# In a seven-product block multiply, the first product is copied by ScalarE into the PSUM bank of another, with two smaller moves around it

## The chip, the cores and the metric

The kernel runs on one NeuronCore of one Trainium2 chip. The metric is device time in microseconds (us) for one execution; lower is better. Three timed runs of the kernel before gave 754.74, 755.83 and 756.22 us; the median, 755.83 us, is what a predicted time is compared with.

## The reference, cut to what matters

The reference is one transformer block: linear attention with a memory, then a gated MLP on its output `h` (2048 rows, 1024 columns). Only the second part matters here:

```
z  = gelu(layernorm(h) @ w_in)            # 2048 x 3584
z1 = z[:, :1792]
z2 = layernorm(z[:, 1792:])               # over the 1792 columns
g  = w_sp @ z2 + b_sp                     # w_sp is 2048 x 2048
out = h + (z1 * g) @ w_out
```

The change lies in the calculation of `z1`, and in the row normalization of `z2` that is done beside it.

## The kernel before, in words

Every instruction is recorded in program order, given to one engine's queue, and supplied with semaphore waits from what it reads and writes (class `_Recorder`, lines 34 to 241; L210, the line all instructions carry in the profile, is the one that emits them). There is no scheduler: each engine runs its instructions strictly in the order in which the code below records them. A whole PSUM bank counts as one cell, so a matmul that adds to a bank waits until every earlier reader of that bank on another engine is done.

**The stage before: z2.** TensorE runs 64 groups of 8 matmuls of 448 columns, ScalarE applies gelu to each (`z2_gelu`, 826), VectorE takes the statistics (`z2_stats`, 830), and GpSimd turns a row's variance into its inverse root with two small instructions (`zrs`, 835 and 836). Side jobs are hung on numbered groups by `at(q, ...)` (994); among them the first weight sums on GpSimd (lines 1016 and 1017).

**The stage of the change: z1, a seven-product block multiply** (`z1_step`, 1199). A 2 x 2 block product is made of seven half-depth products instead of eight. A group `g` (there are 14: 7 column blocks for each of 2 row pairs) has the products 1 to 7; each is four matmuls of 512 columns, with sums of weight blocks as stationary operand (`sz_sum`, 985, GpSimd, tiles `sz`) and differences of activation blocks as moving one (`hn_sum`, 972, VectorE, tiles `ht`). Below, "5 of 9" is product 5 of group 9. A group has three PSUM banks:

- bank 0: product 1, then product 2 added by TensorE; ScalarE applies gelu out of the bank.
- bank 1: product 6, then 7, then 4 added by TensorE.
- bank 2: product 5, then product 3 added.

Product 1 is needed in all four output blocks. The kernel before copies it to SBUF (ScalarE, `s1`, line 1213) and VectorE adds it three times: `u2 = bank 1 + s1` after product 6 (1215); `u3 = bank 1 + s1` and `u3 = bank 2 + u3` after product 7 (1220, 1221); `s1 = bank 1 + s1` after product 4 (1230). A fifth add, `u2 = bank 2 + u2`, comes after product 3 (1233). ScalarE makes each finished block a bf16 block of `z1T` with a gelu (`z1_out`, 1194).

**The order of the products** is written by hand in line 1262:

```
offs = {1: -5, 6: 0, 5: 1, 7: 3, 2: 4, 4: 6, 3: 12}
for x, g, k in sorted((7 * g + offs[k], g, k) for g in range(14) for k in offs):
```

The steady order is 6 of g, 5 of g, 1 of g+1, 7 of g, 2 of g, 3 of g-1, 4 of g, then 6 of g+1. At the opening, where the earlier groups are missing, it is 1, 6, 5 of group 0, 1 of group 1, 7, 2, 4 of group 0, 6 of group 1. Banks are taken in turn from eight (`next_bank`, 421).

The weight sums 1 and 2 of group g+1 are recorded after product 5 of g, sum 3 after product 7, and sum 4 of group g+2 after product 3. The tiles of sums 1 to 3 are single, so sum 1 of a group waits until TensorE has done product 5 of the group before.

**Side jobs of z1** are hung on products by `on(g, k, ...)` (1240). They are: for g of 0 to 7 the normalization of two rows of `z2` (`z2_apply`, 839), one on VectorE after product 6 and one on ScalarE after product 4 (line 1245; the ScalarE form needs a small GpSimd instruction, `znm`, 842, first); in groups 4 to 7 the activation differences of the second row pair; in groups 8, 9 and 11 the scaling of three blocks of `w_sp` on ScalarE, four pieces each, after products 6, 7, 2 and 4 (`sp_part`, 1057, tiles `b11h`, `b12h`, `b22h`); in groups 10 to 13 their differences on VectorE (`sp_sum`, tiles `t1h`, `t2h`, `t3h`). The raw `w_sp` blocks come by transposing DMAs on SP's queue (1250 to 1252).

After z1 comes the gate stage (`gate`, 1087), then the output products.

Of the kernel before, what the change touches and what calls it, by code (L numbers as in the profile page):

```python
# [9 lines left out]
ACTF = mybir.ActivationFunctionType  # L10
ALU = mybir.AluOpType
# [247 lines left out]
def bass_sequential_preLN__memory_aug_infini_attn__mixer_gmlp__prompt_kernel(  # L259
# [17 lines left out]
    pe, act, dve, pool, sp = R.pe, R.act, R.dve, R.pool, R.sp  # L277
# [6 lines left out]
    def tens(name, shape, dt, off):  # L284
        sz = int(np.prod(shape[1:])) * mybir.dt.size(dt)
        assert off % 32 == 0 and off + sz <= ARENA, (name, off, sz)
        t = nc.alloc_sbuf_tensor_at(name, list(shape), dt, offset=abase + off)
        R.space[t[:].tensor.name] = ("sbuf", off)
        return t
# [14 lines left out]
    IDENT = cb("ident", [128, 128], BF16)  # L304
# [73 lines left out]
    ZT = [tens("zt%d" % i, [128, L], F32, o * K) for i, o in enumerate((4, 6, 8, 10, 202, 12))]  # L378
# [30 lines left out]
    PS = nc.alloc_psum_tensor("ps", [128, 8, 512], F32)  # L409
    R.space[PS[:, 0, :].tensor.name] = ("psum", 0)  # L410

    def bank(b):
        return PS[:, b, :]
# [7 lines left out]
    def next_bank():  # L421
        b = rot["banks"][rot["n"] % len(rot["banks"])]
        rot["n"] += 1
        return b
# [367 lines left out]
    for t in range(4):  # L792
        for h in range(2):
            pe.matmul(PS[:, br, t * 128:(t + 1) * 128], RSB[:, h, t:t + 1].to_broadcast([128, 128]), IDENT[:],
                      start=(h == 0), stop=(h == 1))
# [17 lines left out]
    zs, zq, staged = [], [], []  # L813
# [25 lines left out]
    def z2_apply(on_act=False):  # L839
        tc = zq.pop(0)  # L840
        if on_act:
            pool.tensor_scalar(ZNM[:], ZMV[:, tc, 0:1], ZRS[:, 8 * tc:8 * tc + 1], -1.0, ALU.mult, ALU.mult)
            act.activation(Z2H[:, tc, :], Z2[:, tc, :], ACTF.Identity, scale=ZRS[:, 8 * tc:8 * tc + 1], bias=ZNM[:])
            return
        dve.tensor_scalar(Z2H[:, tc, :], Z2[:, tc, :], ZMV[:, tc, 0:1], ZRS[:, 8 * tc:8 * tc + 1], ALU.subtract, ALU.mult)
# [123 lines left out]
    def hb(j, k, p):  # L969
        return HNT[2 * p + k][:, 4 * j:4 * j + 4, :]  # L970
# [7 lines left out]
    def wz_blk(i, j, fc):  # L978
        o = 128 * (fc % 2)
        return WZH[fc // 2][:, 4 * j:4 * j + 4, i, o:o + 128]  # L980

    def sz(g, k):
        return SZ[k - 1 + (k == 4 and g % 2)][:]

    def sz_sum(g, k):
        fc = g % 7
        a, b, op = {1: (wz_blk(1, 0, fc), wz_blk(1, 1, fc), ALU.add), 2: (sz(g, 1), wz_blk(0, 0, fc), ALU.subtract),
                    3: (wz_blk(0, 0, fc), wz_blk(1, 0, fc), ALU.subtract),
                    4: (wz_blk(0, 1, fc), sz(g, 2), ALU.subtract)}[k]
        pool.tensor_tensor(sz(g, k), a, b, op)  # L990
# [3 lines left out]
    def at(q, f, *a):  # L994
        aux.setdefault(q, []).append((f, a))
# [18 lines left out]
    for k in range(4):  # L1014
        at(28 + 2 * k, hn_sum, 1, 1 + k // 2, k % 2)
    for k in (1, 2, 3, 4):
        at(35 + k, sz_sum, 0, k)

    todo = [(0, 2), (0, 3), (0, 8), (0, 9), 0, (0, 10), 1, (0, 11), 2, (1, 0), 3]
    todo += [(1, tc) for tc in range(1, 4)] + [(0, tc) for tc in range(12, NTC)]  # L1020
# [173 lines left out]
    def z1_out(fc, t, src):  # L1194
        act.activation(Z1T[:, fc, t * 512:(t + 1) * 512], src, ACTF.Gelu_apprx_tanh, scale=INV[1][:])

    zb, todo1 = {}, {}

    def z1_step(g, k):
        p, fc = divmod(g, 7)  # L1200
        s1, u2, u3 = ZT[g % 2][:], ZT[2 + g % 3][:], ZT[5][:]
        ka = {1: wz_blk(0, 0, fc), 2: wz_blk(0, 1, fc), 3: sz(g, 4), 4: wz_blk(1, 1, fc), 5: sz(g, 1),
              6: sz(g, 2), 7: sz(g, 3)}[k]
        kb = {1: hb(0, 0, p), 2: hb(1, 0, p), 3: hb(1, 1, p), 4: HT[p][4], 5: HT[p][1], 6: HT[p][2], 7: HT[p][3]}[k]
        first = k in (1, 6, 5)
        r = {1: 0, 2: 0, 6: 1, 7: 1, 4: 1, 5: 2, 3: 2}[k]
        if first:
            zb[g, r] = next_bank()
        b = bank(zb[g, r])
        for i in range(4):  # L1210
            pe.matmul(b, ka[:, i, :], kb[:, i, :], start=(first and i == 0), stop=(i == 3), skip_group_check=True)
        if k == 1:
            act.activation(s1, b, ACTF.Copy)
        if k == 6:
            dve.tensor_tensor(u2, b, s1, ALU.add)
        if k == 5 and g < 13:
            for x in (1, 2):
                sz_sum(g + 1, x)
        if k == 7:
            dve.tensor_tensor(u3, b, s1, ALU.add)  # L1220
            dve.tensor_tensor(u3, bank(zb[g, 2]), u3, ALU.add)
            z1_out(fc + 7, 2 * p + 1, u3)
            if g < 13:
                sz_sum(g + 1, 3)
        if k == 2:
            z1_out(fc, 2 * p, b)
            if g == 0:
                sz_sum(1, 4)
        if k == 4:
            dve.tensor_tensor(s1, b, s1, ALU.add)  # L1230
            z1_out(fc + 7, 2 * p, s1)
        if k == 3:
            dve.tensor_tensor(u2, b, u2, ALU.add)
            z1_out(fc, 2 * p + 1, u2)
            if g < 12:
                sz_sum(g + 2, 4)
        for f, a in todo1.get((g, k), ()):
            f(*a)

    def on(g, k, f, *a):  # L1240
        todo1.setdefault((g, k), []).append((f, a))

    for g in range(8):
        on(g, 6, lambda: zq and z2_apply())
        on(g, 4, lambda: zq and z2_apply(True))
    for k in range(4, 8):
        on(*((4, 6), (5, 6), (6, 6), (7, 6))[k - 4], hn_sum, 1, (1, 2, 3, 4)[k // 2], k % 2)
    on(1, 7, scale_of, 0, 16, None)
# [14 lines left out]
    for x, g, k in sorted((7 * g + offs[k], g, k) for g in range(14) for k in offs):  # L1263
        z1_step(g, k)
# [269 lines left out]
```

## Time and profile before

| What | Value |
|---|---|
| Median of the three timed runs | 755.83 us (754.74 to 756.22) |
| Profiled execution, first to last instruction (span) | 753.7 us; its own device time is not listed, the median stands 2.1 us above the span |
| Granted TensorE clock over the span | 1.000 |
| TensorE matmul busy (PE) | 748.3 us, 99% |
| VectorE busy (DVE) | 557.1 us, 74% |
| ScalarE busy (ACT) | 421.6 us, 56% |
| GpSimd busy (POOL) | 296.3 us, 39% |
| z1 stage | from 404.74 us to about 490.7 us of the span |
| VectorE adds `zt<-ps,zt` | 70, mean 689 ns |
| ScalarE copies `zt<-ps` | 14, median 578 ns |

Times inside the span count from its first instruction. A busy share says how much of the span an engine spent in instructions; a matmul row's duration contains its pipeline, so the distance between the starts of two rows is what TensorE really spends on one. The chain of waits names who released an instruction that had to wait. The lines themselves are shown where the prediction uses them.

### The profile page before, as it was taken

To read this page: it belongs to the slowest core of one execution; us is meant where nothing else is said; L and a number is where in the kernel's file an instruction comes from. 1 tells how busy PE (TensorE), PEld (TensorE's weight loads), DVE (VectorE), ACT (ScalarE), POOL (GpSimd) and SP (SyncE) were. 2 spreads that over 40 slices of the span, in tenths; PEclk is the share of its full clock that TensorE was granted. 3 is DMA by queue.
4 is the path that set the end of the run, shared out by engine and by line. 5 is a ranking of instruction groups with operands and counts; after the bars stand their busy time and mean duration, and the time that the engine had idled before them with its cause. 6 is when DMAs were issued, how large, how long until landed. Compare 5 with 4: busy or idle time off the path is not lost.

```text
span 753.7 us, 13510 instructions
## 1 busy us (share of the span) xinstructions
PE 748.3 (99%) x5470; PEld 359.1 (48%) x5470; DVE 557.1 (74%) x1013; ACT 421.6 (56%) x519; POOL 296.3 (39%) x450
## 2 busy tenths in 40 slices
PE   9999999999999999999999999999999999999998
PEld 4445455555554445545554444444444444444444
DVE  5585589768975576677986796997885385989776
ACT  6777877787777767325894879733231355300000
POOL 2565456555654334010039988622220011222342
PEclk9999999999999999999999999999999999999999
DMA  9554546444523331678650027330019961001211
GB/s 304 171 164 83 96 75 134 99 72 93 120 58 84 119 79 43 162 188 254 192 169 0 1 41 142 56 98 1 0 21 142 262 198 35 0 1 41 79 50 57
DMA packets 136783, 75.09 MB, mean 100 GB/s; under 512 B 98064, under 2 KB 126480, under 8 KB 136720
## 3 DMA queue, kind: packets, MB, share of 16 engines
q1 hardware_dynamic: 129184, 67.14, 37.0%
q10 hardware_dynamic: 7536, 7.08, 3.5%
q8 instruction: 43, 0.70, 0.4%
q14 instruction: 20, 0.16, 0.1%
HBM read 42.74 MB, written 8.39 MB: 68 GB/s over the span
## 4 chain that ended last, share of the span: by engine, by line
PE 90%; DMA 3%; ACT 3%; DVE 2%; POOL 2%; issue 0%; ACTq 0%; DVEq 0%
PE ps L210 90%; DMA sj<-in_B_w_sp_dram 2%; ACT sj L210 2%; POOL zrs L210 1%; DMA wv<-in_A_wv_dram 1%; POOL sz L210 1%; DVE zst L210 1%; ACT z L210 1%; DVE wzh L210 1%; DVE ht L210 0%; DVE zmv L210 0%; ACT L210 0%; DVE fin L210 0%; ACTq L210 0%; DVE top L210 0%
## 5 line engine op out<-in xcount | busy, mean ns | idle before, releaser
L210 ACT ACTIVATE e<-ps 128x2048 bf16<-128x2048 f32 (+1 forms) x96 | 152.6, 1590 | 41.7 <-PE ps L210 41.5
L210 POOL TENSOR_SCALAR_AFFINE_SELECT e<-e 128x512 bf16<-128x512 bf16 x128 | 90.9, 723 | 131.2 <-ACT e L210 131.2
L210 PE MATMUL ps<-win,hnT 128*128 128x448 bf16 x512 | 98.4, 352 | 0.0
L210 POOL TENSOR_TENSOR tmp_s1b<-tmp_s,brow 128x512 f32<-128x512 f32 x28 | 36.4, 1301 | 121.6 <-DVE tmp_u L210 63.0
L210 PEld LDWEIGHTS ps<-win,hnT 128*128 128x128 bf16 x512 | 49.6, 98 | 46.3 <-issue 0.2
L210 PE MATMUL ps<-xnT,wk 128*128 128x512 bf16 x256 | 60.8, 380 | 0.0
L210 DVE TENSOR_TENSOR zt<-ps,zt 128x512 f32<-128x512 f32 x70 | 48.2, 689 | 16.8 <-PE ps L210 13.5
L210 PE MATMUL ps<-xnT,wq 128*128 128x512 bf16 x256 | 60.5, 379 | 0.0
L210 PE MATMUL ps<-wv,xnT 128*128 128x512 bf16 x256 | 60.0, 381 | 0.3 <-DMA wv<-in_A_wv_dram 0.2
L210 PE MATMUL ps<-wo,oT 128*128 128x512 bf16 x256 | 58.0, 379 | 0.0
L210 ACT ACTIVATE z<-ps 128x448 bf16<-128x448 f32 x60 | 30.4, 545 | 33.4 <-PE ps L210 33.4
L210 PE MATMUL ps<-w_out,z1T 128*128 128x512 bf16 x224 | 48.6, 379 | 0.0
L210 DVE BATCH_NORM_STATS2 zst<-z 128x6 f32<-128x448 bf16 x64 | 37.9, 611 | 10.3 <-ACT z L210 10.2
L210 PEld LDWEIGHTS ps<-v,e 128*128 128x128 bf16 x1280 | 38.8, 96 | 14.0 <-issue 6.5
L210 DVE RECIPROCAL rd<-ps 128x16 f32<-128x16 f32 x32 | 8.0, 250 | 47.0 <-PE ps L210 46.8
L210 PE MATMUL ps<-v,e 128*128 128x33 bf16 x1280 | 42.2, 178 | 0.0
L210 ACT ACTIVATE tmp_s<-ps,invy 128x512 f32<-128x512 f32 x7 | 4.8, 688 | 63.3 <-POOL tmp_s1b L210 35.9
L210 POOL TENSOR_TENSOR sz<-wzh 128x512 f16<-128x512 f16 x28 | 34.5, 1232 | 8.3 <-PE ps L210 8.3
L210 PEld LDWEIGHTS ps<-wo,oT 128*128 128x128 bf16 x256 | 24.1, 98 | 27.5
L210 PEld LDWEIGHTS ps<-xnT,wk 128*128 128x128 bf16 x256 | 22.6, 98 | 29.9 <-issue 5.0
L210 ACT ACTIVATE z1T<-zt,inv 128x512 bf16<-128x512 f32 x42 | 29.0, 715 | 13.1 <-DVE zt L210 13.1
L210 PEld LDWEIGHTS ps<-wv,xnT 128*128 128x128 bf16 x256 | 23.1, 98 | 27.3 <-DMA wv<-in_A_wv_dram 0.9
(204 smaller groups left out, 1459.8 us busy)
## 6 DMA issues: line engine op xcount, KB each, us to landing
sj<-in_B_w_sp_dram SPq DMA_DIRECT2D x16, 512.0 KB, 3.7
xch<-in_A_x_dram SPq DMA_DIRECT2D x16, 256.0 KB, 3.7
xr<-in_A_x_dram SPq DMA_DIRECT2D x16, 256.0 KB, 4.0
out_dram<-hch SPq DMA_DIRECT2D x16, 256.0 KB, 2.4
win<-in_B_w_in_dram SPq DMA_DIRECT2D x4, 896.0 KB, 5.3
wz<-in_B_w_in_dram SPq DMA_DIRECT2D x6, 512.0 KB, 8.0
wo<-in_A_wo_dram SPq DMA_DIRECT2D x1, 2048.0 KB, 8.4
fin<-out_dram ACTq DMA_DIRECT2D x16, 128.0 KB, 3.1
```

Of the source, the lines that this page charges most:

```text
L210: ins = getattr(e, op.name)(*op.args, **op.kw)
```

## The change

- `z1_step`: product 1 is copied by ScalarE not to SBUF but into bank 1 of its group (PSUM to PSUM), before product 6; product 6 no longer starts the bank anew but adds onto the copy, and products 7 and 4 add further. Both banks are therefore taken at product 1.
- Where bank 1 had not yet been used with its full 512 columns in this stage (the first three groups), a matmul of 64 columns with the identity is run on its columns 448 to 511 before the copy.
- `u2` after product 6 is a VectorE copy of bank 1, not an add. `u3` is made by a new ScalarE copy of bank 2 after product 5, and after product 7 one VectorE add, `u3 = bank 1 + u3`, replaces two. After product 4 the gelu reads bank 1 directly, without an add. Of five VectorE operations for a group three are left, and ScalarE has six operations in place of five.
- The tile `s1` is gone; `u2` and `u3` have three buffers each.
- The second row normalization of groups 0 to 7 runs on VectorE, not ScalarE; GpSimd's `znm` instructions go with it.
- The four weight sums of group 0 are hung seven z2 groups earlier on GpSimd's queue (numbers 29 to 32, not 36 to 39).

```diff
     for k in (1, 2, 3, 4):
-        at(35 + k, sz_sum, 0, k)
+        at(28 + k, sz_sum, 0, k)
...
-    zb, todo1 = {}, {}
+    zb, todo1, wide = {}, {}, set()
...
-        s1, u2, u3 = ZT[g % 2][:], ZT[2 + g % 3][:], ZT[5][:]
+        u2, u3 = ZT[g % 3][:], ZT[3 + g % 3][:]
...
-        first = k in (1, 6, 5)
         r = {1: 0, 2: 0, 6: 1, 7: 1, 4: 1, 5: 2, 3: 2}[k]
-        if first:
+        if k in (1, 5):
             zb[g, r] = next_bank()
+        if k == 1:
+            zb[g, 1] = next_bank()
         b = bank(zb[g, r])
         for i in range(4):
-            pe.matmul(b, ka[:, i, :], kb[:, i, :], start=(first and i == 0), stop=(i == 3), skip_group_check=True)
+            pe.matmul(b, ka[:, i, :], kb[:, i, :], start=(k in (1, 5) and i == 0), stop=(i == 3),
+                      skip_group_check=True)
+        wide.add(zb[g, r])
         if k == 1:
-            act.activation(s1, b, ACTF.Copy)
+            if zb[g, 1] not in wide:
+                pe.matmul(PS[:, zb[g, 1], 448:512], IDENT[:], IDENT[:, 0:64], start=False, stop=False,
+                          skip_group_check=True)
+            act.activation(bank(zb[g, 1]), b, ACTF.Copy)
         if k == 6:
-            dve.tensor_tensor(u2, b, s1, ALU.add)
+            dve.tensor_copy(u2, b)
+        if k == 5:
+            act.activation(u3, b, ACTF.Copy)
...
         if k == 7:
-            dve.tensor_tensor(u3, b, s1, ALU.add)
-            dve.tensor_tensor(u3, bank(zb[g, 2]), u3, ALU.add)
+            dve.tensor_tensor(u3, b, u3, ALU.add)
             z1_out(fc + 7, 2 * p + 1, u3)
...
         if k == 4:
-            dve.tensor_tensor(s1, b, s1, ALU.add)
-            z1_out(fc + 7, 2 * p, s1)
+            z1_out(fc + 7, 2 * p, b)
...
-        on(g, 4, lambda: zq and z2_apply(True))
+        on(g, 4, lambda: zq and z2_apply())
```

## The prediction

> **What bounds the kernel now.** First the page's busy times: TensorE (PE) is at 99%.
>
> ```profile
> PE 748.3 (99%) x5470; PEld 359.1 (48%) x5470; DVE 557.1 (74%) x1013; ACT 421.6 (56%) x519; POOL 296.3 (39%) x450
> ```
>
> So only two things change the time: TensorE's own work, and gaps in it. Second view, TensorE's waits from 340 to 520 us, which hold the whole stage:
>
> ```profile
> PE ps L210 <- POOL sz L210: 1.0, 1, 1.0
> ```
>
> One wait, for a weight sum of GpSimd. Third view, TensorE's timeline at the opening (start, duration; x4 is one product):
>
> ```profile
> 405.60 1.89 PE L210 MATMUL ps<-z1x,sz 128*128 128x512 f16 x8
> 407.33 1.03 PE L210 MATMUL ps<-hnT,wzh 128*128 128x512 bf16 x4
> ...
> 410.00 1.04 PE L210 MATMUL ps<-z1x,wzh 128*128 128x512 f16 x4
> 412.06 1.90 PE L210 MATMUL ps<-z1x,sz 128*128 128x512 f16 x8 [1.02 <-POOL sz L210]
> ```
>
> Two products lie between 405.60 and 407.33: one takes 0.864 us, and a group of seven 6.05. 4 of 0 starts at 410.00 and should be followed at 410.86; 6 of 1 starts at 412.06. The gap is **1.20 us**. GpSimd's timeline shows why:
>
> ```profile
> 409.09 0.56 POOL L210 TENSOR_TENSOR zrs<-zrs,mhz 128x1 f32<-128x1 f32 x1
> 409.61 1.16 POOL L210 TENSOR_TENSOR sz<-wzh 128x512 f16<-128x512 f16 x1
> 410.85 1.16 POOL L210 TENSOR_TENSOR sz<-sz,wzh 128x512 f16<-128x512 f16 x1
> ```
>
> Sum 2 of group 1 ends at 412.01 and releases TensorE; before it GpSimd was behind with the `zrs` pairs. From there to 490 us the starts follow at 0.864, and TensorE loses some 0.1 us in all. Everything else in the stage is hidden, so the question is what the new order puts in TensorE's way.
>
> **Sums sooner: -1.20 us.** The four sums of group 0 (4 x 1.15 = 4.6 us, at 397.37 to 404.53 in GpSimd's queue) go to where GpSimd mostly waits for VectorE's `zmv` (its first `zrs` waited 13.4 us, to 387.9). The last `zmv` came at 406.43, its pair 0.9 us later: GpSimd is free at about 407.4, not 409.6. Sum 1 of group 1 still waits for product 5 of 0, at about 408.4 with the new wait below; two sums of 1.16 end at 410.8. Product 6 of 1 is due at 411.7. The lead is 0.9 us and the wait goes.
>
> **Copy ahead of product 6: +0.87 at the opening, nothing later.** At the opening product 6 follows product 1 directly. The copy that product 6 will now wait for is this row:
>
> ```profile
> 405.80 0.60 ACT L210 ACTIVATE zt<-ps 128x512 f32<-128x512 f32 x1 [0.32 <-PE ps L210]
> ```
>
> It ends at 406.40, with 0.05 for the release 406.45, where product 6 started at 405.60: 0.85, and 0.02 for the identity matmul that the copy follows. No row copies PSUM to PSUM. The nearest are 0.578 (`zt<-ps`, PSUM to SBUF) and 0.592 (`ps<-z1T`, SBUF to PSUM); if the two sides added up it would be 1.17. I take 0.60, near both; range of this term 0.8 to 1.45. From group 1 on four products (3.46 us) lie between 1 and 6, less 0.6 of copy and 0.2 of pipeline and releases: ScalarE may be 2.6 us late. Below it stays within that.
>
> **Three identity matmuls: +0.15.** The nearest row is the 16-column `ps<-sqb,ones` at 415.53: the next matmul starts 0.03 later, its busy time is 0.17 and a weight load 0.10. So 0.03 to 0.27 each; 0.05 taken.
>
> **ScalarE's new copy of bank 2: +2.0.** This is what the change adds without showing it. Before, product 4 waited only for VectorE's first add, which read the old `s1`. Now the add that frees bank 1 for product 4 needs `u3`, a ScalarE copy made after product 5. Queued ahead of that copy, in groups 8, 9 and 11, are the `w_sp` pieces. ScalarE's timeline there:
>
> ```profile
> 457.89 1.14 ACT L210 ACTIVATE b11h<-b11r,sc 128x1024 f16<-128x1024 bf16 x1
> 458.93 0.58 ACT L210 ACTIVATE zt<-ps 128x512 f32<-128x512 f32 x1
> 459.51 0.72 ACT L210 ACTIVATE z1T<-zt,inv 128x512 bf16<-128x512 f32 x1
> 460.13 1.13 ACT L210 ACTIVATE b11h<-b11r,sc 128x1024 f16<-128x1024 bf16 x1
> 461.17 0.67 ACT L210 ACTIVATE z1T<-ps,inv 128x512 bf16<-128x512 f32 x1
> 461.75 1.14 ACT L210 ACTIVATE b11h<-b11r,sc 128x1024 f16<-128x1024 bf16 x1
> 462.79 1.32 ACT L210 ACTIVATE z1T<-zt,inv 128x512 bf16<-128x512 f32 x2
> 464.01 1.13 ACT L210 ACTIVATE b11h<-b11r,sc 128x1024 f16<-128x1024 bf16 x1
> 465.05 1.14 ACT L210 ACTIVATE b12h<-b12r,sc 128x1024 f16<-128x1024 bf16 x1
> 466.09 0.58 ACT L210 ACTIVATE zt<-ps 128x512 f32<-128x512 f32 x1
> ```
>
> Starts are 1.04 apart after a piece, 0.62 after a gelu from SBUF, 0.57 after one from PSUM. ScalarE never rests, and the last row copies a product (1 of 10) that TensorE had finished at 463.1: 3.0 us late. That was free: the first matmul behind it, 7 of 10 at 469.08, needed only VectorE's add of 466.69 to 467.38.
>
> I walk this with the new order, in the times of before:
>
> - **Group 8.** Without the eight 1.87 us normalizations ScalarE arrives on time: first piece at 455.2, the copies by 457.3, then it waits for 7 of 8.
> - **Group 9.** 7 of 8 starts at 456.99 and is readable at 458.02. VectorE's add 458.07 to 458.76, the gelu from 458.81. To the copy of bank 2 of group 9 there stand gelu 0.62, piece 1.04, gelu 0.57, piece 1.04, two gelus 1.19, two pieces 2.08: 6.54 (before: 459.51 to 466.09, 6.58). Copy at 465.35, done 465.93, add 465.98 to 466.67, product 4 at 466.72. It was due at 465.63: **1.1**.
> - **Group 10.** The gelu after that add starts at 466.72; 5.5 (only the first piece of group 9 lies ahead of it) to the next copy, then 0.58 + 0.69 + 0.15 of releases: 6.9, against a group of 6.05: **0.85**.
> - **Group 11.** No pieces in group 10, one after: 0.62 + 0.57 + 0.62 + 0.57 + 1.04 + 1.42 = 4.8, under 6.05: nothing.
> - **Group 12.** As group 9 with one piece less: 1.1 - 1.04, **0.05**, perhaps 0.3 with VectorE's `t3h` in the way.
>
> Sum 2.0. Both ends: 0 if ScalarE is never late, 2.4 with group 12's 0.3 and 0.05 more in the others. I take the walk, since its intervals are rows of this stage.
>
> **VectorE and the second normalization: 0.** Groups 4 to 7 are VectorE's fullest with normalization: 5.58 busy of 6.04 us from 442.32 to 448.36. Out go five adds of 0.69, in come a copy (0.28 for 132 columns, 0.69 for an add of 512: I take 0.66), two adds and 0.74: 4.9 us. Its slack is the cover; without it the delay falls on product 7, whose bank the copy must leave within 1.5 us of product 6.
>
> A `sz` sum lasts 1.15 alone and up to 1.49 where VectorE's `ht` or `z2h` runs beside it; sum 2 ended at 447.31 where its product began at 448.36, a lead of 1.05. One more 0.34 is within it: nothing. The Trainium skill's "SBUF — State Buffer" (Who interferes with whom) speaks against this move: VectorE in its two-port modes holds the ports it shares with GpSimd for the whole instruction, and GpSimd stops. By that rule alone each added normalization would cost a sum its full 0.74, and the total would still stand, with 0.3 of lead left.
>
> **Sum.** -1.20 + 0.87 + 0.15 + 2.0 = **+1.8 us** on the span of 753.7, so 755.5; no gap stands after the stage to take it back (TensorE is at 99% to the end, granted clock 1.000). The median stands 2.1 above the span: **757.7 us**.
>
> **Rivals.**
>
> - *ScalarE is not late* (ends as no change, or a little faster). One mechanism: the copy of bank 2 in groups 9 and 10 comes within 1.9 us of product 5. It decides at the chain of 6.54: below 5.4 it costs nothing. Then -1.20 + 0.87 + 0.15 = -0.2: 755.6. For it: lags of 3.0 us cost nothing before. Against: then 1.7 us were left to product 7 (467.38 to 469.08), now product 4 is the first behind, and the 1.04 intervals are steady.
> - *The opening keeps its wait.* GpSimd's sums of group 1 stay late, held by product 5 or VectorE's normalizations. The 0.9 us of lead speak against; if it fails wholly, +1.2: 758.9.
> - *The PSUM copy is slow*, 1.17 not 0.60: +0.6 at the opening, and a later queue in between: 758.3 to 758.6.
>
> **How the numbers follow.** Chances: forecast 0.58, ScalarE not late 0.17, opening keeps its wait 0.15, slow copy 0.08, other 0.02. The difference that a measurement of this kernel can tell from no change is 0.2%, 1.5 us: 754.3 to 757.3. Of the forecast about 0.13 falls below 757.3, since its own error is some 0.6 us; of the first rival 0.13 is within and 0.04 below. Slower 0.68, same 0.26, faster 0.06. The range runs from the first rival less 0.4, 755.2, to 759.3, the second rival with 0.4 of other ends.
>
> **What would show it.** TensorE's waits after: no `sz`; one of about 0.9 us for ScalarE's `ps` at 405.6; two of about 1.1 and 0.85 for VectorE's `zt` near 466 and 473. ScalarE's rows: a copy into `ps` of about 0.6. Wrong if the `zt` waits are absent (first rival), if `sz` stays, or if waits appear in groups 1 to 7.

## The result, and the profile after

| | Before | After |
|---|---|---|
| Median | 755.83 us (754.74 to 756.22, 5 runs) | 758.93 us (758.39 to 759.31, 5 runs) |
| Ratio to before, 95% interval | | 1.0044 [1.0033, 1.0055] |
| Span of the profiled execution | 753.7 us | 757.2 us |
| z1 stage: first product's start to the gate's first matmul | 404.74 to 490.76: 86.0 us | 405.10 to 494.29: 89.2 us |
| Gate's first matmul to the last matmul's start | 260.0 us | 260.0 us |

The change made the kernel slower by 3.1 us, 0.44%. The stage alone accounts for it: 3.2 us longer, with nothing lost or won after it. The remaining 0.4 us between the two spans stands ahead of the stage (404.74 against 405.10) and is scatter: in the runs below the stage starts between 404.6 and 405.4 by their rows. In the same way the 2.1 us that the prediction found between median and span is no fixed distance: every run with both numbers stands 1.7 to 1.8 us above its span, so the profiled execution before was one of some 0.4 us under the median.

TensorE is busy for 748.9 us after the change, against 748.3; nearly all of what was lost is in its waits.

TensorE's waits from 340 to 520 us (who waited for whom, total, times, longest). The one line for `sz` is gone, and two others stand there:

```profile
PE ps L210 <- DVE zt L210: 2.5, 4, 1.0
PE ps L210 <- ACT ps L210: 0.7, 1, 0.7
```

This view counts from the modelled end of the matmul before, so it is smaller than the gap between starts. The gaps, from TensorE's timeline after, first at the opening:

```profile
405.10 1.03 PE L210 MATMUL ps<-hnT,wzh 128*128 128x512 bf16 x4
405.96 0.19 PE L210 MATMUL ps<-ident 128*128 128x64 bf16 x1
406.83 1.90 PE L210 MATMUL ps<-z1x,sz 128*128 128x512 f16 x8 [0.67 <-ACT ps L210]
```

and later in the stage (the rows with a wait are product 4 of groups 4, 6, 9 and 10; the row at 466.17 is product 3 of group 8, just ahead of product 4 of group 9):

```profile
436.15 1.04 PE L210 MATMUL ps<-z1x,wzh 128*128 128x512 f16 x4 [0.48 <-DVE zt L210]
448.89 1.04 PE L210 MATMUL ps<-z1x,wzh 128*128 128x512 f16 x4 [0.48 <-DVE zt L210]
...
466.17 1.03 PE L210 MATMUL ps<-hnT,sz 128*128 128x512 bf16 x4
468.15 1.04 PE L210 MATMUL ps<-ht,wzh 128*128 128x512 f16 x4 [0.96 <-DVE zt L210]
...
474.99 1.04 PE L210 MATMUL ps<-ht,wzh 128*128 128x512 f16 x4 [0.62 <-DVE zt L210]
```

A product takes 0.864 us. From 405.10 the next should start at 405.96 and starts at 406.83: **0.87 us**. From 466.17 the next is due at 467.03 and starts at 468.15: **1.12 us**. Read in the same way, the gaps are 0.65 in group 4, 0.65 in group 6, 1.12 in group 9, 0.78 in group 10 and 0.19 in group 12. With the opening, 0.05 for the two identity matmuls outside it and -1.19 for the wait that went, they make +3.12 us. The stage is 3.17 longer.

### The profile page after: what moved, and what is told of

Same layout as the page of the kernel before. It is cut to its first block, busy times and chain, and to the rows that moved or that the text cites. A ratio compares the mean times of both kernels' runs of the same rounds, so it can differ in the third digit from the quotient of the medians.

```text
span 757.2 us, 13482 instructions
## 1 busy us (share of the span) xinstructions
PE 748.9 (99%) x5473; PEld 358.9 (47%) x5473; DVE 551.7 (73%) x993; ACT 416.0 (55%) x525; POOL 295.2 (39%) x442
## 4 chain that ended last, share of the span: by engine, by line
PE 94%; ACT 2%; DVE 2%; DMA 1%; issue 1%; ACTq 0%; DVEq 0%
PE ps L210 94%; DMA wv<-in_A_wv_dram 1%; DVE zt L210 1%; DVE z2h L210 1%; ACT z1T L210 1%; ACT b12h L210 1%; ACT b11h L210 0%; ACT zt L210 0%; ACT L210 0%; DVE fin L210 0%; ACT ps L210 0%; ACTq L210 0%; DVEq L220 0%; DVE ht L210 0%; ACTq L209 0%
## 5 line engine op out<-in xcount | busy, mean ns | idle before, releaser
L210 POOL TENSOR_TENSOR sz<-wzh 128x512 f16<-128x512 f16 x28 | 36.2, 1294 | 22.7 <-PE ps L210 13.6
L210 ACT ACTIVATE qk<-ps 128x512 bf16<-128x512 f32 x48 | 28.8, 599 | 12.5 <-PE ps L210 12.5
L210 ACT ACTIVATE sj<-sj 128x2048 bf16<-128x2048 bf16 x16 | 30.6, 1916 | 9.0 <-DMA sj<-in_B_w_sp_dram 8.8
```

What stands on the lines that cost most here:

```text
L210: ins = getattr(e, op.name)(*op.args, **op.kw)
```

## The experiments

The theory after the result: three causes that add up. (A) At the opening product 6 waits for the copy of product 1. (B) In groups 9, 10 and 12 product 4 waits for VectorE's add, that for ScalarE's copy of bank 2, and that stands behind the `w_sp` pieces. (C) In groups 4 and 6 VectorE is late because a normalization takes twice its time beside GpSimd's sums. The rivals: VectorE's own queue is the cause in groups 9 to 12 too; in groups 4 and 6 it is the number of its instructions and not their length; the waits trade with one another, so that undoing any part brings nothing.

### Second normalization back on ScalarE

```diff
-        on(g, 4, lambda: zq and z2_apply())
+        on(g, 4, lambda: zq and z2_apply(True))
```

> The changed kernel with the second row normalization back on ScalarE. Three waits of TensorE are to be told apart: 0.87 us at the opening (copy of product 1), 0.65 us each in groups 4 and 6, and 1.12, 0.78 and 0.19 us at product 4 of groups 9, 10 and 12. Theory (ScalarE's queue sets the last three, VectorE's normalizations the two in groups 4 and 6): the two of 0.65 go, but ScalarE enters group 8 late by the normalization of 1.87 us that is back on it, so product 4 waits some 0.3 us in group 8 and 1.9 in group 9, 0.85 in group 10, 0.2 in group 12; gaps of the stage 4.2 us in all against 3.6 of the changed kernel, time about 759.4. Rival (the waits of groups 9 to 12 come of VectorE's queue, which is emptier here): they shrink from 2.1 us or stay, time 757.6 or less.

Measured: 758.84 us, ratio 1.004 [1.0027, 1.0054]. The gaps in groups 4 and 6 are gone, and product 4 waits 0.45 us in group 8, 1.82 in group 9, 0.78 in group 10 and 0.19 in group 12, all close to the expectation. The time is 0.6 us under the expected 759.4 because the expectation counted 3.6 us of gaps for the changed kernel, where its rows add up to 4.26; this run's add up to 4.11.

ScalarE's timeline as it enters group 8 shows the cause: the normalization stands ahead of the first piece, and that ahead of the copy of bank 2.

```profile
455.21 1.88 ACT L210 ACTIVATE z2h<-z,znm,zrs 128x1792 f16<-128x1792 bf16 x1
457.00 1.13 ACT L210 ACTIVATE b11h<-b11r,sc 128x1024 f16<-128x1024 bf16 x1
458.04 0.57 ACT L210 ACTIVATE zt<-ps 128x512 f32<-128x512 f32 x1
```

With VectorE relieved and ScalarE loaded, the waits of groups 8 and 9 grew (0 and 1.12 in the changed kernel). That is theory B, against its rival: VectorE's add in group 9 does not stand behind other work of VectorE, it waits 4.50 us for ScalarE's copy here and 3.80 in the changed kernel. Undoing the move of the normalization is thus worth next to nothing by itself: it takes away 1.29 us of waits and gives back 1.14.

### Copy of bank 2 on VectorE

```diff
-            act.activation(u3, b, ACTF.Copy)
+            dve.tensor_copy(u3, b)
```

> The changed kernel with the copy of bank 2 after product 5 made by VectorE, not ScalarE. Theory: with ScalarE out of the way of product 4 the waits of 1.12, 0.78 and 0.19 us in groups 9, 10 and 12 go (-2.1). VectorE gets 0.6 us more for each group, and in groups 4 to 7, where it already waits, that comes out as waits of about 0.5 us in each of the four (2.0 in place of 1.3). Gaps of the stage about 2.9 to 3.2, time 757.9 to 758.3. Rival (VectorE itself is late in groups 9 and 10): those waits stay or grow, time over 759.5.

Measured: 758.83 us, ratio 1.0039 [1.0026, 1.0053]. The three gaps of groups 9, 10 and 12 are gone altogether: B is shown from the other side. Groups 4 to 7 now lose 1.43, 0.25, 1.44 and 0.25 us. Their sum, 3.4, is more than the 2.0 expected, so the time is 0.5 to 0.9 us above the expected range. The mechanism held and its size did not: the expectation had put the same wait in all four groups, and a normalization is not equally long in each. The two that stand ahead of the add for product 4 read 1.54 and 1.60 us in group 4, 1.71 and 1.69 in group 6, but 0.73 or 0.74 in groups 5 and 7, where the gaps are small.

### No weight sums for groups 5 to 8

```diff
-        if k == 5 and g < 13:
+        if k == 5 and g < 13 and not 4 <= g <= 7:
...
-            if g < 13:
+            if g < 13 and not 4 <= g <= 7:
                 sz_sum(g + 1, 3)
...
-            if g < 12:
+            if g < 12 and not 3 <= g <= 6:
                 sz_sum(g + 2, 4)
```

> The changed kernel without the weight sums of groups 5 to 8 (their products use older sums, so this part of the calculation is left out). GpSimd then rests where VectorE runs the normalizations of groups 4 to 7. Theory (the normalization takes 1.4 to 1.7 us there, not 0.74, because GpSimd's sums hold the ports that both share): all normalizations of groups 4 to 7 take 0.74 us, the two waits of 0.65 us in groups 4 and 6 go, the others stay; time 1.3 less than the changed kernel, about 757.6. Rival (VectorE has simply too many instructions in these groups, or the row's duration is a wait for something else): durations or the two waits stay, time about 758.9.

Measured: 757.19 us, ratio 1.0016 [1.0006, 1.0026]; 1.7 us below the changed kernel, where 757.6 was expected; the gaps give 1.3 of it, as expected. First VectorE's timeline of the changed kernel, then GpSimd's beside it:

```profile
430.27 1.54 DVE L210 TENSOR_SCALAR z2h<-z,zmv,zrs 128x1792 f16<-128x1792 bf16 x1
431.74 0.68 DVE L210 COPY zt<-ps 128x512 f32<-128x512 f32 x1
432.34 1.60 DVE L210 TENSOR_SCALAR z2h<-z,zmv,zrs 128x1792 f16<-128x1792 bf16 x1
433.86 1.64 DVE L210 TENSOR_TENSOR ht<-hnT 128x1024 f16<-128x1024 bf16 x1
435.42 1.28 DVE L210 TENSOR_TENSOR zt<-ps,zt 128x512 f32<-128x512 f32 x2
```

```profile
430.18 1.16 POOL L210 TENSOR_TENSOR sz<-wzh,sz 128x512 f16<-128x512 f16 x1
432.30 1.15 POOL L210 TENSOR_TENSOR sz<-wzh 128x512 f16<-128x512 f16 x1 [0.96 <-PE ps L210]
433.53 1.41 POOL L210 TENSOR_TENSOR sz<-sz,wzh 128x512 f16<-128x512 f16 x1
```

and VectorE's timeline in the run without those sums:

```profile
429.59 1.54 DVE L210 TENSOR_SCALAR z2h<-z,zmv,zrs 128x1792 f16<-128x1792 bf16 x1
431.05 0.68 DVE L210 COPY zt<-ps 128x512 f32<-128x512 f32 x1
431.65 0.73 DVE L210 TENSOR_SCALAR z2h<-z,zmv,zrs 128x1792 f16<-128x1792 bf16 x1
432.30 0.68 DVE L210 TENSOR_TENSOR ht<-hnT 128x1024 f16<-128x1024 bf16 x1
433.37 0.69 DVE L210 TENSOR_TENSOR zt<-ps,zt 128x512 f32<-128x512 f32 x1 [0.39 <-PE ps L210]
```

The first normalization still has a sum beside it (sum 4 of group 4, from 429.49 to 430.64, which the edit leaves in) and takes 1.54. From the second on GpSimd rests: 0.73 in place of 1.60, `ht` 0.68 in place of 1.64, and the add that frees product 4 no longer comes at 435.42 after three slow instructions but waits for its product. Both gaps of 0.65 are gone and those of groups 9, 10 and 12 stand as before. The order and number of VectorE's instructions are the same in both kernels, so their number alone is not the cause: theory C. This run shortens `ht` as well, so by itself it does not tell the normalizations from `ht`. The changed kernel's own rows do: `ht` takes 1.64 or 1.65 us in all four groups, while the two normalizations ahead of the add for product 4 take 1.54 and 1.60 in group 4 and 1.71 and 1.43 in group 6, which have the gaps, and 1.50 and 0.74 in group 5 and 1.49 and 0.74 in group 7, which have none.

### The kernel before with one line of the change

```diff
-        at(35 + k, sz_sum, 0, k)
+        at(28 + k, sz_sum, 0, k)
```

> The kernel before with one line of the change: the weight sums of group 0 seven z2 groups sooner. Theory: the wait of 1.20 us for the second sum of group 1 goes and nothing takes its place, since product 1 is still copied to SBUF: gaps of the stage under 0.3 us, time 754.6, ratio 0.9984. Rival (another wait takes its place, as in the changed kernel with 0.87 us): 755.5.

Measured: 754.62 us, ratio 0.9989 [0.998, 0.9998], as forecast. TensorE's timeline at the opening:

```profile
410.06 1.04 PE L210 MATMUL ps<-z1x,wzh 128*128 128x512 f16 x4
410.93 1.89 PE L210 MATMUL ps<-z1x,sz 128*128 128x512 f16 x8
```

Product 6 of group 1 follows after 0.87, not after 2.06 as in the kernel before. The stage is 1.2 us shorter. This is the fastest kernel of the study, and the difference is just clear of the measurement.

### Both later costs undone

The two edits above, of the normalization and of the copy of bank 2, together.

> The changed kernel with both later costs undone: the second normalization back on ScalarE, the copy of bank 2 after product 5 on VectorE. What stays is the copy of product 1 into product 6's bank and the earlier weight sums. Theory (three separate causes that add): normalizations on VectorE take 0.74 us again, no waits in groups 4 to 12; the 0.87 us at the opening stays; gaps of the stage about 1.1 us, time 755.5, ratio 0.9997. Rival (the causes trade with one another, as in the two runs that undid one each): waits of over 1 us come back in groups 4 to 10, time over 757.

Measured: 755.76 us, ratio 1.0001 [0.9992, 1.0011], where 755.5 was expected. The normalizations left on VectorE in groups 4 to 7 take 0.74 us again. The opening keeps its 0.87; groups 4 to 7 lose 0.17 to 0.18 each, which was not expected (VectorE's `ht`, 1.64 us there, stands ahead of its copy of bank 2); no gap over 0.1 elsewhere. The two undone parts, each worth nothing alone, are worth some 3 us together. So the rival, by which the waits would come back somewhere else, falls. But the edits do not simply add, as the theory had it: each alone moved work onto the engine at which the other cost stands, and made that one larger by as much as it saved.

### And products 5 and 6 of group 0 changed in order

```diff
-        if k == 5 and g < 13:
+        if k == (5 if g else 6) and g < 13:
...
-    for x, g, k in sorted((7 * g + offs[k], g, k) for g in range(14) for k in offs):
+    for x, g, k in sorted((7 * g + offs[k] - 2 * (g == 0 and k == 5), g, k) for g in range(14) for k in offs):
```

> As the kernel that keeps only the copy into product 6's bank and the earlier sums, with products 5 and 6 of group 0 changed in order, so that product 5 covers the copy of product 1 at the opening. Theory: the 0.87 us shrinks to under 0.1, no other wait of over 0.15 us in the stage, time 754.6, the same as the kernel before with sums sooner alone (754.62). Rival (sums 1 and 2 of group 1, now released one product later, bring the wait for the weight sum back): 0.5 us or more at product 6 of group 1, time 755.2 or more.

Measured: 755.24 us, ratio 0.9997 [0.9987, 1.0006]. The interval holds no change, and the time fits the rival's "755.2 or more", so the time decides nothing; the trace does. The opening copy is covered, as expected, and no wait for a sum comes back, but product 4 of group 0 now waits 0.47 us. VectorE's and TensorE's timelines of this run:

```profile
408.60 1.69 DVE L210 TENSOR_SCALAR z2h<-z,zmv,zrs 128x1792 f16<-128x1792 bf16 x1
410.21 0.68 DVE L210 TENSOR_TENSOR zt<-ps,zt 128x512 f32<-128x512 f32 x1
```

```profile
410.95 1.04 PE L210 MATMUL ps<-z1x,wzh 128*128 128x512 f16 x4 [0.30 <-DVE zt L210]
```

The first normalization came beside sum 1 of group 1 (408.66 to 409.81), took 1.69 us, though by its row it began 0.06 us ahead of the sum, and stood ahead of the add that frees bank 1. Neither the expectation nor its rival had it; it is cause C at another place. With the 0.18 in each of four groups, it is why this kernel does not reach the 754.62 of the one line alone.

## Why the prediction was right or wrong

The direction held, and 758.93 lies in the range of 755.2 to 759.3; of the 3.1 us lost the forecast had 1.9 (757.7). That the time lies in the range is in part luck. The range reached so high for the rival in which the opening keeps its wait, priced at 758.9; that wait went, and a cost which the sum had put at nothing took its place. By the prediction's own sign, waits in groups 1 to 7, this part of it was wrong: product 4 waits 0.65 us in groups 4 and 6.

- **Sums sooner, -1.20.** Right: the `sz` wait is gone after the change, and the one line alone took 1.2 us off the stage and 1.1 off the median (754.62 against 755.69 for the kernel before on the same chip).
- **Copy ahead of product 6, +0.87.** Right: 0.87. The copy into PSUM takes 0.58 us, within 0.02 of the 0.60 taken; the slow-copy rival falls.
- **Identity matmuls, +0.15.** 0.02 to 0.03 each, some 0.08 for the three; the one at the opening is in the 0.87 already, so the sum counts it twice.
- **ScalarE's copy of bank 2, +2.0.** Right, by group too: forecast 1.1, 0.85 and 0.05 to 0.3, measured 1.12, 0.78 and 0.19. ScalarE's timeline after is the walk, and VectorE's add of group 9, which frees product 4, waits for its end:

```profile
460.26 0.72 ACT L210 ACTIVATE z1T<-zt,inv 128x512 bf16<-128x512 f32 x1 [1.08 <-DVE zt L210]
460.88 1.13 ACT L210 ACTIVATE b11h<-b11r,sc 128x1024 f16<-128x1024 bf16 x1
461.92 0.67 ACT L210 ACTIVATE z1T<-ps,inv 128x512 bf16<-128x512 f32 x1
462.49 1.14 ACT L210 ACTIVATE b11h<-b11r,sc 128x1024 f16<-128x1024 bf16 x1
...
465.75 1.14 ACT L210 ACTIVATE b12h<-b12r,sc 128x1024 f16<-128x1024 bf16 x1
466.79 0.58 ACT L210 ACTIVATE zt<-ps 128x512 f32<-128x512 f32 x1
```

```profile
467.40 1.29 DVE L210 TENSOR_TENSOR zt<-ps,zt 128x512 f32<-128x512 f32 x2 [3.80 <-ACT zt L210]
```

  From the gelu at 460.26 to the copy at 466.79 are 6.53 us, against 6.54 in the sum. The rival "ScalarE is not late" falls with it.
- **VectorE and the second normalization, 0.** This is the step that failed: it cost 1.3 us. The prediction counted 0.74 us for a normalization, a row that in the kernel before, from group 3 on, always began while no sum was running. VectorE's and GpSimd's timelines before:

```profile
413.75 0.97 DVE L210 TENSOR_SCALAR z2h<-z,zmv,zrs 128x1792 f16<-128x1792 bf16 x1
...
425.86 0.74 DVE L210 TENSOR_SCALAR z2h<-z,zmv,zrs 128x1792 f16<-128x1792 bf16 x1
```

```profile
426.16 1.45 POOL L210 TENSOR_TENSOR sz<-wzh 128x512 f16<-128x512 f16 x1 [0.71 <-PE ps L210]
```

  The row at 425.86 stands for those of groups 3 to 7. The row at 413.75 was a sign that went unread: a sum ran until 414.23, and the same instruction took 0.97 us. The prediction weighed the shared ports in one direction only, as a delay of GpSimd's sums, and found 1.05 us of lead for those. In the other direction, where a sum is running when VectorE's instruction begins, VectorE is the one that waits: eight normalizations between 424 and 458 us took 1.38 to 1.71 us. Its slack in groups 4 to 7 was computed with 0.74 for both, and where both were long, in groups 4 and 6, it was not there. The delay also fell on product 4 and not, as the prediction had it, on product 7. The Trainium skill's "SBUF — State Buffer" (Who interferes with whom) does state both directions: who issues first has the ports, and the other blocks. The runs agree, with 1.60 against 0.73 us for the same instruction with and without a sum beside it; that it is ports which the two engines share is the page's word, the runs show only the delay.
- **The opening keeps its wait** (rival): no. Sum 2 of group 1 ended at 411.49 and its product began at 412.14, 0.65 us later (0.9 in the prediction; sum 1 took 1.45 us, beside VectorE's normalization, and not 1.16).

## What to carry to other kernels

When a copy is moved to another engine, ask which matmul is first behind it, and walk that engine's queue up to it with the starts of its own rows, side jobs included: an engine that was 3 us late for free is not free for a copy that releases a bank within 2 us. A duration taken from a profile holds only for the company that the instruction had there; before it is used on VectorE at a new place, look whether GpSimd will be running. When two parts that are undone one by one bring nothing, undo them together before either is called harmless.

## What the runs showed of the hardware

- In the changed kernel a normalization on VectorE that began during a GpSimd sum ended 0.48 to 0.49 us after that sum (431.81 after 431.34, 438.11 after 437.62, 450.84 after 450.36). Two that began 0.11 us ahead of a sum's end waited for the following sum too: from 443.01 to 444.72, beside sums ending at 443.12 and 444.23, and from 455.75 to 457.46, beside sums ending at 455.86 and 456.97.
- The `ht` differences of groups 4 to 7, which read 1.64 us in both kernels, take 0.68 us where the sums are left out. So over half of that row, which looked like the cost of the instruction, was waiting.
- ScalarE's copy of 512 columns takes 0.58 to 0.60 us from PSUM to PSUM and as much from PSUM to SBUF, by the rows of the changed kernel: the target made at most 0.02 us of difference.
